# Gated attention followed by an FFT gate, on one core: scores emitted in bursts of four tiles, a halved filter spectrum kept in SBUF, and a tail in borrowed buffers

## The chip, the cores and the metric

The kernel runs on one core of a Trainium2 chip. The metric is the device time of one execution in microseconds (us), as the median of several executions. The unchanged kernel took 1450.63 us (median of 3, 1443.97 to 1451.0) when the prediction was made.

## The reference, cut to what matters

```python
# batch 8, S = 3136 rows (49 * 64), D = 256, d_qk = 64
def attention(u, v, z):
    scores = matmul(z, z.T) / S                 # S x S per batch
    attn = maximum(scores, 0) ** 2
    return u * matmul(attn, v)                  # becomes x

def gate(x, w_proj, filter_fft, w_out):
    x1, x2, x3 = split(x @ w_proj, 3)
    X2 = rfft(x2, n=S, axis=1)
    H = rfft(filter_fft, n=S, axis=0)
    y = x1 * irfft(X2 * H, n=S, axis=1) * x3
    return y @ w_out                            # float32
```

The kernel computes in bf16 with f32 accumulation. Scores are symmetric in z, so they can be made transposed, ready to be multiplied with v. The transform of length 3136 is done as matrix products: a first stage, a second stage, a product with the filter's spectrum, and the way back (stages 3 and 4). The batches are taken in four pairs for it.

## The kernel before

One "chunk" is a group of 384 to 512 output rows of one batch: 8 batches times 7 chunks are 56 chunks. One chunk has 13 "steps". A step makes two 128-row tiles of scores (`scores`), squares the positive part, and multiplies the tiles of some steps earlier with v (`values`) into one accumulator in PSUM, `psout`. At the end of a chunk `finish_chunk` multiplies the accumulator with u into `xT`, and three projections use it. All other work of TensorE (projections, transposes, the transform) is "background": pieces in a queue that are put between the steps.

```python
LAG = 3
class Load:                       # greedy choice of the engine for a piece
    def cost(self, eng, n, fast=1.0):
        if eng == "act": return 150.0 + n / 1.2
        if eng == "dve": return 120.0 + n / 0.96 / fast
        return 200.0 + 2.15 * n
    def take(self, n, engines, fast=1.0):
        best = min(engines, key=lambda e: self.t[e] + self.cost(e, n, fast))
        self.t[best] += self.cost(best, n, fast)
        return best
# ... rring 3 buffers (R), aring 6 (A), psum 3 pairs of banks, psacc 1 (psout) ...

    def stage2(p, kb):            # per block: load y, load the filter's spectrum, multiply
        yl = load_y(y_d[p], kb)
        hl = hld.tile([P, 2, KB * D], BF16, name="hl")
        nc.sync.dma_start(out=hl[:Q2], in_=h_d[:, kb])        # 392 KB
        # ... two matmuls into ps, evicted to xs ...
        nc.vector.tensor_tensor(tt[:Q2], xs[:Q2].unsqueeze(1).to_broadcast(...), hl[:Q2], ALU.mult)

    def scores(b, c, i):
        # ...
            for j in range(2):
                hs = ds(N1 * j, N1)                           # 64 of the 128 rows
                nc.tensor.matmul(ps[:, j, :cw], zT[hs, ds((2 * i + j) * P, P)], zT[hs, ds(s0, cw)],
                                 start=True, stop=True)
        # ...
        if load.take(k * cw, ("act", "dve")) == "act":
            nc.scalar.activation(Rv, pv, AF.Relu)
        else:
            nc.vector.tensor_single_scalar(Rv, pv, 0.0, ALU.max)
        eng = load.take(k * cw, ("act", "dve", "pool"))       # the square
        if eng == "act":
            nc.scalar.activation(Av, Rv, AF.Square)
        else:
            (nc.vector if eng == "dve" else nc.gpsimd).tensor_tensor(Av, Rv, Rv, ALU.mult)
        return A

    inv_s2 = 1.0 / float(S) ** 2
    def finish_chunk(b, c):
        for dh in range(2):       # xT = psout * uT, two DVE operations
            nc.vector.scalar_tensor_tensor(xT[:, dh, :cw], po[:, dh, :cw], inv_s2, uT[:, dh, :cw],
                                           ALU.mult, ALU.mult)

    def plan(b, c):
        # own: the three projections of the chunk just finished, transposes of the next u and z
        # rest: this chunk's share of far (the pieces of the transform)
        for j, f in enumerate(own):
            mixed.append(f)
            lo, hi = j * len(rest) // n, (j + 1) * len(rest) // n
            mixed += rest[lo:hi]
        # ...

    for gi in range(len(steps) + LAG):
        if gi < len(steps):
            amap[steps[gi]] = scores(*steps[gi])
        owed[0] += rate[0]
        while owed[0] >= 1.0 and near:
            near.popleft()()                                  # a background piece
            owed[0] -= 1.0
        # ...
        if gi >= LAG:
            b, c, i = steps[gi - LAG]
            values(b, c, i, amap.pop((b, c, i)))
            if i == NST - 1:
                finish_chunk(b, c)
                while near:
                    near.popleft()()
                plan(b, c)
    # tail: what is left in near and far
```

In the tail, the last pair's transform remains: its whole first stage, stages 2 and 3 in 16 blocks, stages 4 and 5 (load, gate, output projection, store). All loads and stores of the transform go through the SyncE queue.

Of the kernel before, what the change touches and what calls it, by code (L numbers as in the profile page):

```python
# [26 lines left out]
LAG = 3  # L27


class Load:  # L30
# [5 lines left out]
    def cost(self, eng, n, fast=1.0):  # L36
        if eng == "act":
            return 150.0 + n / 1.2
        if eng == "dve":
            return 120.0 + n / 0.96 / fast  # L40
        return 200.0 + 2.15 * n
# [8 lines left out]
def kernel(  # L50
# [37 lines left out]
    h_d = dram.tile([Q2, NKB, 2, KB * D], BF16, name="h_d")  # L88

    const = ctx.enter_context(tc.tile_pool(name="const", bufs=1))  # L90
    zpool = ctx.enter_context(tc.tile_pool(name="zpool", bufs=2))
    zinp = ctx.enter_context(tc.tile_pool(name="zinp", bufs=1))
    uinp = ctx.enter_context(tc.tile_pool(name="uinp", bufs=3))
    utp = ctx.enter_context(tc.tile_pool(name="utp", bufs=2))
    vpool = ctx.enter_context(tc.tile_pool(name="vpool", bufs=9))
    rring = ctx.enter_context(tc.tile_pool(name="rring", bufs=3))
    aring = ctx.enter_context(tc.tile_pool(name="aring", bufs=6))
    psum = ctx.enter_context(tc.tile_pool(name="psum", bufs=3, space=bass.MemoryType.PSUM))
    psacc = ctx.enter_context(tc.tile_pool(name="psacc", bufs=1, space=bass.MemoryType.PSUM))

    def ps_tile():
        return psum.tile([P, 2, 512], F32, tag="ps", name="ps")

# [25 lines left out]
    def load_z(b):  # L129
        zin = zinp.tile([P, NT, dqk], BF16, name="zin")  # L130
        for h, n in split_h(0, NT):
            nc.gpsimd.dma_start(out=zin[ds(N1 * h, N1), 0:n, :], in_=rows_view(z[b], h, 0, n))
        zd = zinp.tile([P, NT, 2, dqk], BF16, name="zd")
        nc.vector.tensor_copy(zd[:, 0:NT - 1], zin[:, 0:NT - 1].unsqueeze(2).to_broadcast([P, NT - 1, 2, dqk]))
        nc.vector.tensor_copy(zd[:N1, NT - 1], zin[:N1, NT - 1].unsqueeze(1).to_broadcast([N1, 2, dqk]))
        zins[b] = zd
        zTs[b] = zpool.tile([P, S], BF16, name="zT")

    def tr_z(b, t0, n):
        zd, zT = zins[b], zTs[b]  # L140
        ps = psum.tile([P, 2048], BF16, tag="ps", name="psz")
        w = 0
        for t in range(t0, t0 + n):
            r = rows_of(t)
            nc.tensor.transpose(ps[:, ds(w, r)], zd[:r, t].rearrange("p a d -> p (a d)"), ident[:r, :r])
            w += r
        evac(zT[:, ds(t0 * P, w)], ps[:, :w], w, fast=2.0)
# [34 lines left out]
    load_z(0)  # L182
    load_v(0, 0)
    load_u(0, 0)
    for q in range(1, 7):
        load_v(0, q)
    wp16 = const.tile([P, 2, 3 * D], BF16, name="wp16")
    nc.gpsimd.dma_start(out=wp16[:], in_=moe_w_proj.rearrange("(t p) n -> p t n", p=P))
    wo16 = const.tile([P, 2, D], BF16, name="wo16")
    nc.gpsimd.dma_start(out=wo16[:], in_=moe_w_out.rearrange("(t p) n -> p t n", p=P))  # L190


    T = const.tile([P, NT, 2, P], BF16, name="T")
    C = const.tile([P, N2, 2, N1], BF16, name="C")
    NTAB = 5
# [5 lines left out]
    with tc.tile_pool(name="tabs", bufs=1) as tabs:  # L201
        pi = tabs.tile([P, 1], I32, name="pi")
        nc.gpsimd.iota(pi[:], pattern=[[0, 1]], base=0, channel_multiplier=1)
        pf = tabs.tile([P, 1], F32, name="pf")
        nc.vector.tensor_copy(pf[:], pi[:])

        def reduced(src, shape, add, name):
            q = tabs.tile(shape, F32, name="q_" + name)
            r = tabs.tile(shape, F32, name="r_" + name)
            if add:  # L210
                nc.vector.tensor_single_scalar(r[:], src, float(add), ALU.add)
                src = r[:]
            nc.vector.tensor_scalar(q[:], src, 1.0 / S, RND, ALU.mult, ALU.add)
            nc.vector.tensor_single_scalar(q[:], q[:], RND, ALU.subtract)
            nc.vector.scalar_tensor_tensor(r[:], q[:], -float(S), src, ALU.mult, ALU.add)
            return r

        ki = tabs.tile([P, NT, N1], I32, name="ki")
        nc.gpsimd.iota(ki[:], pattern=[[0, NT], [1, N1]], base=0, channel_multiplier=0)
        ti = tabs.tile([P, NT, N1], I32, name="ti")  # L220
        nc.gpsimd.iota(ti[:], pattern=[[1, NT], [0, N1]], base=0, channel_multiplier=N2)
        hi = tabs.tile([P, 1], F32, name="hi")
        nc.vector.tensor_single_scalar(hi[:], pf[:], float(N1), ALU.is_ge)
        nc.vector.tensor_single_scalar(hi[:], hi[:], float(HT - N2 * N1), ALU.mult)
        kf = tabs.tile([P, NT * N1], F32, name="kf")
        nc.vector.tensor_copy(kf[:], ki[:].rearrange("p a b -> p (a b)"))
        tf = tabs.tile([P, NT * N1], F32, name="tf")
        nc.vector.tensor_copy(tf[:], ti[:].rearrange("p a b -> p (a b)"))
        nc.vector.scalar_tensor_tensor(kf[:], tf[:], hi[:, 0:1], kf[:], ALU.add, ALU.mult)
        for add, name in ((QUART, "c"), (0, "s")):  # L230
            r = reduced(kf[:], [P, NT * N1], add, name)
            r3 = r[:].rearrange("p (a b) -> p a b", a=NT)
            if add:
                nc.scalar.activation(T[:, :, 0, 0:N1], r3, AF.Sin, scale=SIN_SCALE)
                nc.scalar.activation(T[:, :, 1, N1:P], r3, AF.Sin, scale=SIN_SCALE)
            else:
                nc.scalar.activation(T[:, :, 0, N1:P], r3, AF.Sin, scale=-SIN_SCALE)
                nc.scalar.activation(T[:, :, 1, 0:N1], r3, AF.Sin, scale=SIN_SCALE)


        nf = tabs.tile([P, 1], F32, name="nf")
        nc.vector.tensor_scalar(nf[:], pf[:], 0.5, -0.25, ALU.mult, ALU.add)
        nc.vector.tensor_single_scalar(nf[:], nf[:], RND, ALU.add)
        nc.vector.tensor_single_scalar(nf[:], nf[:], RND, ALU.subtract)
        par = tabs.tile([P, 1], F32, name="par")
        nc.vector.scalar_tensor_tensor(par[:], nf[:], -2.0, pf[:], ALU.mult, ALU.add)
        dpos = tabs.tile([P, 1], F32, name="dpos")
        nc.vector.tensor_single_scalar(dpos[:], par[:], float(QUART), ALU.mult)
        dneg = tabs.tile([P, 1], F32, name="dneg")
        nc.vector.tensor_single_scalar(dneg[:], par[:], -float(QUART), ALU.mult)  # L250
        k2i = tabs.tile([P, N2], I32, name="k2i")
        nc.gpsimd.iota(k2i[:], pattern=[[N1, N2]], base=0, channel_multiplier=0)
        nk = tabs.tile([P, N2], F32, name="nk")
        nc.vector.tensor_copy(nk[:], k2i[:])
        nc.vector.tensor_scalar(nk[:], nk[:], nf[:, 0:1], None, ALU.mult)
        ph = tabs.tile([P, NTAB, N2, 2], F32, name="ph")
        offs = (
# [251 lines left out]


    far = deque()

    def queue_filter():
        filt = {}

# [139 lines left out]
```

## Time and profile before

| | before |
|---|---|
| time, median | 1450.63 us |
| profiled span | 1451.7 us |
| end of the last values matmul | 1293.6 us |
| tail after it | 158.1 us |
| TensorE busy, mean granted clock | 86%, 0.939 |

The first lines are from the profile page of the kernel before: busy time of the engines, then three rows of 40 equal slices of the span, in which a digit is the busy share, the granted TensorE clock, or the DMA share in tenths (9 is 90% or more). PE is TensorE, PEld its weight loads (which overlap PE), DVE is VectorE, ACT ScalarE, POOL GpSimd and SP SyncE.

```profile
span 1451.7 us, 20110 instructions
...
PE 1245.9 (86%) x7379; PEld 562.1 (39%) x7379; DVE 960.5 (66%) x933; ACT 852.7 (59%) x953; POOL 800.7 (55%) x655
...
PE   3888999999988989999989999999999989985643
PEclk8999999999999999999999999999999999995566
DMA  7323543332354625664344725662354535545667
```

There are three stages. In the head TensorE waits for its first data, in the main stage it is busy nearly always, and in the last four slices it is not, at a low clock, while the DMA share rises.

The costliest groups of the page say what TensorE waits for. The columns are line, engine, operation, output<-input, form, count | busy us, mean ns of one | idle us before them, and what ended most of that idle time.

```profile
L496 PE MATMUL psout<-A,vt 128*128 128x512 bf16 (+3 forms) x2800 | 664.0, 359 | 25.2 <-DVE A L483 11.6
...
L465 PE MATMUL ps<-zT 64*128 64x512 bf16 (+2 forms) x1344 | 255.3, 360 | 4.0 <-ACT R L474 1.6
L483 DVE TENSOR_TENSOR A<-R 128x1024 bf16<-128x1024 f32 (+5 forms) x141 | 204.3, 1449 | 81.7 <-ACT R L474 81.4
...
L421 PE MATMUL ps<-xT,wp_142 128*128 128x512 bf16 (+2 forms) x448 | 118.1, 369 | 72.5 <-DVE xT L506 70.0
```

The projections (L421) sat idle for 72.5 us, of which `xT` from DVE ended 70.0 us. No other TensorE group waits that long.

Busy TensorE is not TensorE at its peak. The timeline of the kernel before shows matmuls in order of time: start in us, us, engine, line, operation, tiles, form, how many in a row.

```profile
602.45 0.81 PE L496 MATMUL psout<-A,vt 128*128 128x384 bf16 x4
603.19 0.34 PE L465 MATMUL ps<-zT 64*128 64x384 bf16 x2
603.46 0.51 PE L164 MATMUL psu<-ident,uin 128*128 128x128 bf16 x6
```

The durations overlap, so starts are what counts. Four values matmuls of 384 columns take 4 x 0.163 = 0.65 us between one another, but the score pair starts 0.74 us after the first. The two score matmuls use 64 rows of the array each and run beside each other in 0.17 us, but the next 128-row matmul starts after 0.27 us. Every change between 64-row and 128-row matmuls costs about 0.1 us more than the stream itself. Over the main stage the median extra is 96.5 ns, and in the order of the instructions there are 1415 such changes up to the last values matmul.

The next lines are from the same timeline at the end of a chunk. The number in brackets is idle time before the instruction, and its releaser.

```profile
441.52 0.32 PE L465 MATMUL ps<-zT 64*128 64x384 bf16 x1
443.28 0.34 PE L421 MATMUL ps<-xT,wp_142 128*128 128x384 bf16 x1 [1.44 <-DVE xT L506]
...
444.75 1.49 PE L496 MATMUL psout<-A,vt 128*128 128x384 bf16 x4
...
447.31 1.04 PE L496 MATMUL psout<-A,vt 128*128 128x384 bf16 x4
```

After the last values matmul only one score pair covers the making of `xT`, so TensorE stands still for 1.44 us.

The tail, by window. The columns are stretch, length, then busy us and count for TensorE, weight loads, DVE, ACT, POOL, then granted clock, DMA share, GB/s. The stretches are: to the first second-stage matmul; to the last third-stage matmul; to the first load of stage 4 used; to the end.

```profile
1293.60:1324.10 30.50, 12.50 (x116) 7.58 (x115) 8.79 (x9) 9.04 (x10) 0.00 (x0) 0.68 0.52 141
1324.10:1383.10 59.00, 39.26 (x96) 15.91 (x96) 26.77 (x22) 25.25 (x25) 0.00 (x0) 0.62 0.62 193
1383.10:1388.90 5.80, 0.03 (x1) 0.04 (x1) 0.00 (x0) 1.02 (x1) 0.00 (x0) 0.50 0.28 84
1388.90:1451.70 62.80, 25.18 (x198) 18.41 (x198) 15.18 (x14) 12.87 (x13) 0.00 (x0) 0.69 0.78 193
```

No engine is full in the tail. The first stage of the last pair is still to be done there, the middle loads 392 KB of spectrum per block, and the last part issues all its loads and stores from one queue.

### The profile page before, as it was taken

How to read it: one execution, taken by the hardware profiler on the slowest of the kernel's cores; microseconds unless marked ns; L12 is line 12 of the kernel's file. 1: busy time of each engine (PE TensorE's matmuls, PEld its weight loads, DVE VectorE, ACT ScalarE, POOL GpSimd, SP SyncE). 2: the span in 40 equal slices, each digit the busy share in tenths (PEclk: the TensorE clock that was granted, in tenths of full speed). 3: DMA queues.
4: the chain of work that ended last, by engine and by line, in shares of the span. 5: the costliest groups of instructions: out<-in, count | busy, mean ns of one | idle time of the engine just before them, and what ended most of it. 6: DMA issues, size and time to landing. Idle time of an engine off the chain costs nothing. (4 is left out here: it accounts for less than half of the span.)

```text
span 1451.7 us, 20110 instructions
## 1 busy us (share of the span) xinstructions
PE 1245.9 (86%) x7379; PEld 562.1 (39%) x7379; DVE 960.5 (66%) x933; ACT 852.7 (59%) x953; POOL 800.7 (55%) x655
## 2 busy tenths in 40 slices
PE   3888999999988989999989999999999989985643
PEld 1233433443343334543334334543344334542222
DVE  7766677667767776667767766676777866653421
ACT  3655666666665556666666656666666656653421
POOL 8656765576555655556656855565566755530000
PEclk8999999999999999999999999999999999995566
DMA  7323543332354625664344725662354535545667
GB/s 119 70 65 79 141 118 94 91 64 51 85 137 121 144 75 142 150 128 89 99 122 132 177 69 144 157 140 64 92 136 136 140 97 143 136 106 176 204 170 182
DMA packets 164900, 173.69 MB, mean 120 GB/s; under 512 B 18496, under 2 KB 119040, under 8 KB 164800
## 3 DMA queue, kind: packets, MB, share of 16 engines
q1 hardware_dynamic: 144656, 141.35, 34.3%
q0 software_dynamic: 20144, 31.05, 14.7%
q8 instruction: 58, 0.95, 0.3%
q14 instruction: 42, 0.34, 0.1%
HBM read 129.50 MB, written 73.86 MB: 140 GB/s over the span
## 5 line engine op out<-in xcount | busy, mean ns | idle before, releaser
L483 POOL TENSOR_TENSOR A<-R 128x768 bf16<-128x768 f32 (+3 forms) x398 | 663.4, 1673 | 426.9 <-ACT R L474 262.1
L496 PE MATMUL psout<-A,vt 128*128 128x512 bf16 (+3 forms) x2800 | 664.0, 359 | 25.2 <-DVE A L483 11.6
L474 ACT ACTIVATE R<-ps 128x1024 f32<-128x1024 f32 (+4 forms) x474 | 416.1, 886 | 275.7 <-PE ps L465 229.6
L496 PEld LDWEIGHTS <-vt 128*128 128x128 bf16 (+1 forms) x2800 | 251.3, 99 | 267.2 <-issue 97.6
L476 DVE TENSOR_SCALAR R<-ps 128x1024 f32<-128x1024 f32 (+3 forms) x254 | 264.7, 1048 | 125.4 <-PE ps L465 107.0
L465 PE MATMUL ps<-zT 64*128 64x512 bf16 (+2 forms) x1344 | 255.3, 360 | 4.0 <-ACT R L474 1.6
L483 DVE TENSOR_TENSOR A<-R 128x1024 bf16<-128x1024 f32 (+5 forms) x141 | 204.3, 1449 | 81.7 <-ACT R L474 81.4
L481 ACT ACTIVATE A<-R 128x1024 bf16<-128x1024 f32 (+4 forms) x189 | 177.8, 941 | 89.6 <-DVE R L476 87.0
L421 PE MATMUL ps<-xT,wp_142 128*128 128x512 bf16 (+2 forms) x448 | 118.1, 369 | 72.5 <-DVE xT L506 70.0
L465 PEld LDWEIGHTS <-zT 64*128 64x128 bf16 x1344 | 67.0, 93 | 249.6 <-issue 243.5
L351 DVE TENSOR_TENSOR tt<-xs,hl 98x2048 bf16<-98x2048 bf16 x64 | 100.2, 1567 | 48.9 <-ACT xs L108 43.3
L388 DVE TENSOR_TENSOR yT<-ps,gl 128x1024 bf16<-128x1024 f32 x48 | 58.7, 1222 | 57.4 <-DMA gl<-g_d_64 31.5
L153 POOL DMA_DIRECT2D uin<-in_u_dram x112 | 63.9, 573 | 44.0 <-PE psu L164 37.5
L421 PEld LDWEIGHTS <-wp_142 128*128 128x128 bf16 x448 | 38.7, 99 | 117.3 <-DVE xT L506 59.6
L360 PE MATMUL ps<-tt,FT 98*98 98x512 bf16 x256 | 80.6, 443 | 4.0 <-DVE tt L351 4.0
L108 ACT ACTIVATE ve<-ps 98x1024 bf16<-98x1024 f32 x49 | 50.0, 1021 | 35.8 <-PE ps L360 35.4
L506 DVE SCALAR_TENSOR_TENSOR xT<-psout,uT 128x512 bf16<-128x512 f32 (+2 forms) x112 | 64.8, 615 | 8.3 <-PE psout L496 8.2
L347 PE MATMUL ps<-yl,FT 98*98 98x512 bf16 x128 | 46.8, 449 | 26.2 <-DMA yl<-y_d_68 24.3
L108 ACT ACTIVATE xs<-ps 98x1024 bf16<-98x1024 f32 x45 | 46.0, 1021 | 38.6 <-PE ps L347 38.3
L108 ACT ACTIVATE ot<-ps 128x1024 f32<-128x1024 f32 (+1 forms) x35 | 34.5, 985 | 56.4 <-PE ps L404 20.9
L404 PE MATMUL ps<-wo_144,yT 128*128 128x256 bf16 (+1 forms) x400 | 57.0, 285 | 11.5 <-DVE yT L393 7.1
L174 POOL DMA_DIRECT2D vt<-in_v_dram x104 | 56.9, 554 | 15.3 <-PE ps L465 11.5
(324 smaller groups left out, 935.9 us busy)
## 6 DMA issues: line engine op xcount, KB each, us to landing
hl<-h_d SPq DMA_DIRECT2D x64, 392.0 KB
out_dram<-ot SPq DMA_DIRECT2D x192, 128.0 KB
vt<-in_v_dram POOLq DMA_DIRECT2D x96, 128.0 KB, 4.4
uin<-in_u_dram POOLq DMA_DIRECT2D x56, 128.0 KB, 3.5
h_d<-hl SPq DMA_DIRECT2D x16, 392.0 KB
uin<-in_u_dram POOLq DMA_DIRECT2D x56, 96.0 KB, 2.9
yl<-y_d_69 SPq DMA_DIRECT2D x16, 196.0 KB
yl<-y_d_65 SPq DMA_DIRECT2D x16, 196.0 KB
```

The lines of the kernel that those rows point to most:

```text
L108: nc.scalar.activation(dst, src, AF.Copy)
L153: nc.gpsimd.dma_start(out=uin[ds(N1 * h, N1), 0:m, :], in_=rows_view(u[b], h, t0, m))
L351: nc.vector.tensor_tensor(tt[:Q2], xs[:Q2].unsqueeze(1).to_broadcast([Q2, 2, KB * D]), hl[:Q2], ALU.mult)
L360: nc.tensor.matmul(ps[:Q2, j, :], m, tt[:Q2, i, ds(j * 512, 512)], start=(i == 0), stop=(i == 1))
L421: nc.tensor.matmul(ps[:, nb, :cw], wp16[:, ks, ds((2 * comp + nb) * P, P)], xT[:, ks, :cw], start=(ks == 0), stop=(ks == 1))
L465: nc.tensor.matmul(ps[:, j, :cw], zT[hs, ds((2 * i + j) * P, P)], zT[hs, ds(s0, cw)], start=True, stop=True)
L474: nc.scalar.activation(Rv, pv, AF.Relu)
L476: nc.vector.tensor_single_scalar(Rv, pv, 0.0, ALU.max)
L481: nc.scalar.activation(Av, Rv, AF.Square)
L483: (nc.vector if eng == "dve" else nc.gpsimd).tensor_tensor(Av, Rv, Rv, ALU.mult)
L496: nc.tensor.matmul(po[:, dh, :cw], vts[b, kt // 4][:r, kt % 4, ds(dh * P, P)], A[:r, kt - 2 * i, :cw], start=(kt == 0), stop=(kt == NT - 1))
L506: nc.vector.scalar_tensor_tensor(xT[:, dh, :cw], po[:, dh, :cw], inv_s2, uT[:, dh, :cw], ALU.mult, ALU.mult)
```

## The change

The intent has five parts.

1. Scores are emitted two steps at a time (four tiles), then two values steps, so that TensorE changes between 64-row and 128-row matmuls half as often. `LAG` goes from 3 to 4, the ring of `A` from 6 to 8 buffers.
2. At a chunk end, transform pieces come ahead of the projections. Squares are no longer given to DVE.
3. The spectrum of the real filter is symmetric, so only half of it is made (9 blocks for 16). It stays in SBUF, and is read backwards through three extra tables.
4. The first stage of a pair's transform is done chunk by chunk, as soon as the chunk's projection is there. The tables are made behind the first chunk's scores, where they stood ahead of them.
5. In the tail, loads go through POOL's queue into buffers of the attention that are free by then, and `psout` serves as a fourth PSUM buffer.

The core of the diff (cuts marked with `# ...`):

```diff
-LAG = 3
+LAG = 4
+NH = N1 // 2 + 1
# ... cost(): act 150 -> 190 + n/1.2, dve 120 -> 150 + n/0.96
# ... pools: uinp 3 -> 2, vpool 9 -> 8, x2p 17 -> 10, aring 6 -> 8, gp 2 -> 3, no h_d, no x1p
+    tail = {"on": False, "n": 0}
     def ps_tile():
+        if tail["on"]:
+            tail["n"] += 1
+            if tail["n"] % 4 == 0:
+                return psacc.tile([P, 2, 512], F32, name="psout")
         return psum.tile([P, 2, 512], F32, tag="ps", name="ps")
+    def buf(shape, dtype, own, name, lent):
+        if tail["on"]:
+            p, tag = lent
+            return p.tile(shape, dtype, tag=tag, name=name)
+        return late[own].tile(shape, dtype, name=name)
+    def dma_in(**kw):
+        (nc.gpsimd if tail["on"] else nc.sync).dma_start(**kw)
# ... tables() is now a function and the last piece of the first plan; T, FT changed
     def stage2(p, kb):
-        hl = hld.tile([P, 2, KB * D], BF16, name="hl")
-        nc.sync.dma_start(out=hl[:Q2], in_=h_d[:, kb])
# ...
-        nc.vector.tensor_tensor(tt[:Q2], xs[:Q2]..., hl[:Q2], ALU.mult)
+        nc.vector.tensor_tensor(tt[:Q2], xs[:Q2]..., late["H"][:Q2, :, ds(a0, KB), :]..., ALU.mult)
# ... scores():
-        eng = load.take(k * cw, ("act", "dve", "pool"))
+        eng = load.take(k * cw, ("act", "pool"))
# ... plan(): the share of the transform is put ahead of each own piece
-        for j, f in enumerate(own):
-            mixed.append(f)
-            lo, hi = j * len(rest) // n, (j + 1) * len(rest) // n
-            mixed += rest[lo:hi]
+        for j in range(n):
+            hi = -(-(j + 1) * len(rest) // n)
+            near.extend(rest[done:hi])
+            done = hi
+            near.extend(own[j:j + 1])
# ... own also gets first_stage(b, c) for the second batch of a pair
-    for gi in range(len(steps) + LAG):
-        if gi < len(steps):
-            amap[steps[gi]] = scores(*steps[gi])
# ...
+    for g0 in range(0, total + LAG, 2):
+        for s in (g0, g0 + 1):
+            if s < total:
+                amap[s] = scores(*steps[s])
+        vs = [s for s in (g0 - LAG, g0 + 1 - LAG) if 0 <= s < total]
+        if len(vs) == 2 and steps[vs[1]][2] == NST - 1:
+            vs.reverse()
+        if vs and steps[vs[0]][2] != NST - 1 or not vs:
+            background(1.0)
+        for j, s in enumerate(vs):
+            # ... values(); at a chunk's last one finish_chunk, rest of near, plan
+            if j == 0:
+                background(1.0)
+    tail["on"] = True
```

## The prediction

> **What bounds it now.** TensorE, in three stages (per-slice and window views). Head, 0 to 44 us: PE mostly waits for tables and first squares. Main, 44 to 1294 us: PE busy 46 to 47 of 50 us, clock 0.98. Tail, 1294 to 1451 us: 157 us, PE at most 60% busy, clock 0.61 to 0.67.
>
> I split the main stage's 1250 us by start-to-start times of matmuls (timeline). Streaming (N/2.4 ns plus 2.5): 965 us. Mode changes: a 64-row score matmul starts 312 ns after a values matmul instead of 216 (N=512), 258 instead of 163 (N=384); the way back costs 103 ns more than its stream. The Trainium skill, "TensorEngine Tiling (Array Packing)", Key Properties, says that changing the tiling mode drains the array; the trace agrees, at about 100 ns a change. Some 1,400 changes: 140 us. Waits: 145 us, of which 69 us is the first projection waiting for xT at 56 chunk ends (costliest groups: 72.5 us idle there, released by xT). The other 76 us includes the clock.
>
> **What the change does.**
>
> 1. Two score steps in a row, then two values steps; stage-1 pieces often follow scores. By instruction order, mode changes fall from 1,418 to 892. 526 x 0.1 us = **-52 us**, all critical.
> 2. At a chunk end, four score matmuls and a background piece (0.9 us) stand between the last values matmul and the first user of xT, where one score pair stood. An xT takes two DVE operations of 0.55 to 0.68 us. 69 falls to 20 us: **-49 us**.
> 3. Streaming is unchanged: half the filter's second stage goes (-7 us), pair 3's first stage moves in from the tail (+5 us).
> 4. DVE loses its 141 squares (204 us) but takes back relus; ACT, DVE and POOL carry 700 to 940 us each, 65 to 80% of the shorter main stage. Three PSUM pairs serve bursts of two scores: **+10 to +30 us** of new short waits.
> 5. Head: tables come behind the first chunk, first scores need half of z. Table-making (20 us of DVE) still blocks the filter's first stage: **-5 us**.
> 6. Tail: the first stage (23 us) shrinks to two units. Stage 2/3 took 65 us, waiting 2.4 to 4.9 us for y loads behind 392 KB spectrum loads; without them, with eight load buffers, a chain of about 2.3 us a block: 40 us. In stage 4/5 (66 us) the SP queue issues almost without a gap (100 issues of 0.4 to 0.75 us). Half move to POOL. The skill, "DMA: Bandwidth & Descriptors", Issuing engines are not separate DMA queues, says spreading issues only saves sequencer time; engines are already 76% busy, so 12 us comes. Tail 157 to 112: **-45 us**.
>
> **Prediction.** 1450 - 52 - 49 + 20 - 5 - 45 = 1319, say 1315 us. Range 1270 to 1350. Faster by over 2%: 0.96; within: 0.03; slower: 0.01.
>
> **What would show it.** Right: score groups of four with one pair of changes; idle before the first projection under 25 us; values end near 1200 us; tail 105 to 120 us, DMA share above 0.8 in its second half. Wrong: PE idle before background matmuls released by evictions over 100 us; values waiting for POOL squares; POOL's in-order queue stuck on load issues.
>
> **What would make it wrong.** PSUM turnover eating the saved drains; the xT wait moving to the next values matmul, which needs the one accumulator; a lower clock.

## The result, and the profile after

| | before | after |
|---|---|---|
| time, median of the same rounds | 1449.78 us (1443.97 to 1451.0, 4 runs) | 1298.0 us (1296.0 to 1299.69, 4 runs) |
| profiled span | 1451.7 us | 1294.2 us |
| last values matmul ends | 1293.6 us | 1185.7 us |
| tail | 158.1 us | 108.5 us |
| mean granted clock | 0.939 | 0.965 |

The ratio is 0.896, with a 95% interval of 0.8931 to 0.8989. Ratios here are the mean time of one kernel's fast runs over that of the other's fast runs of the same rounds, so they are not quite the ratio of the medians quoted.

The same lines of the profile page, of the kernel after:

```profile
span 1294.2 us, 19775 instructions
...
PE 1164.2 (90%) x7285; PEld 553.6 (43%) x7349; DVE 888.5 (69%) x936; ACT 845.4 (65%) x954; POOL 844.1 (65%) x746
...
PE   6499999999999989999999999999999989997754
PEclk9699999999999999999999999999999999999677
DMA  8144342225233455667223456667222445655548
```

This trace lacks 64 of 7349 matmul records, as the two counts for PE and PEld show. Counts of mode changes below are therefore taken from the order of the instructions. The costliest groups of the kernel after, with the same columns as before:

```profile
L541 PE MATMUL psout<-A,vt 128*128 128x512 bf16 (+4 forms) x2750 | 643.7, 355 | 27.1 <-DVE xT L551 23.5
...
L508 PE MATMUL ps<-zT 64*128 64x512 bf16 (+2 forms) x1344 | 197.4, 358 | 15.0 <-DVE R L519 10.5
...
L464 PE MATMUL ps<-xT,wp_167 128*128 128x384 bf16 (+2 forms) x430 | 104.9, 356 | 11.0 <-ACT R L517 3.3
```

The wait of the projections went from 72.5 to 11.0 us, and `xT` is no longer what ends most of it. The values matmuls now wait 23.5 us for `xT`, but 13.0 us of that is one single wait in the head, told of below. The scores wait a little more for relus, 15.0 us where they waited 4.0.

The timeline of the kernel after:

```profile
608.40 0.61 PE L508 MATMUL ps<-zT 64*128 64x512 bf16 x4
608.94 1.04 PE L541 MATMUL psout<-A,vt 128*128 128x512 bf16 x4
```

Four score matmuls now share one way in and one way out. From the first of them to the values matmul is 0.54 us: two pairs of 0.216 us, and once 0.1 us. The size of a drain is as it was (median extra 95.5 ns), but the number up to the last values matmul is 888 where it was 1415.

The tail after, with the windows and columns as before:

```profile
1185.70:1198.20 12.50, 4.16 (x31) 1.98 (x30) 3.18 (x5) 2.79 (x4) 8.59 (x14) 0.82 0.72 216
1198.20:1240.90 42.70, 32.81 (x96) 15.04 (x96) 23.89 (x20) 26.44 (x27) 10.88 (x18) 0.73 0.51 157
1240.90:1247.80 6.90, 0.04 (x1) 0.04 (x1) 0.00 (x0) 1.02 (x1) 2.66 (x4) 0.54 0.22 69
1247.80:1294.20 46.40, 24.88 (x198) 19.10 (x198) 15.18 (x14) 12.88 (x13) 19.45 (x28) 0.72 0.80 216
```

Three parts gave 18.0, 16.3 and 16.4 us, and the short gap between them cost 1.1 us.

The two spans differ by 157.5 us, and the parts of that are:

| part | before to after |
|---|---|
| streaming of matmuls up to the last values (from shapes and counts; of the kernel after in a complete trace, that of the run `after_tailsp`) | -2 us |
| mode changes, 1415 to 888 at 0.0965 us | -51 us |
| all other stalls up to the last values, waits and half clock (what is left of the difference) | -54 us |
| first matmul, 7.6 to 6.7 us | -1 us |
| tail | -50 us |

The third row is the net of several. Idle time of TensorE in the main stage (from the end of the second chunk) waiting for `xT` went from 71.6 to 12.9 us, idle time for all else from 21 to 34 us, and time at half clock from 51 to 10 us, which is worth about half of that in work, 20 us. These come to some 66 us, more than the row, since the terms overlap. In the head there is a new wait of 13 us, but up to the second `xT` the head as a whole is only 1.2 us longer (77.4 us for 76.2).

### The profile page after: what moved, and what is told of

It reads as the page before. It is cut to its first block, busy times and chain, and to the rows that moved or that the text cites. A ratio compares the mean times of both kernels' runs of the same rounds, so it can differ in the third digit from the quotient of the medians.

```text
span 1294.2 us, 19775 instructions
## 1 busy us (share of the span) xinstructions
PE 1164.2 (90%) x7285; PEld 553.6 (43%) x7349; DVE 888.5 (69%) x936; ACT 845.4 (65%) x954; POOL 844.1 (65%) x746
## 4 chain that ended last, share of the span: by engine, by line
PE 39%; DVE 5%; DMA 4%; POOL 3%; issue 3%; ACT 2%; SPq 1%; DVEq 0%; ACTq 0%; POOLq 0%
PE psout L541 18%; PE ps L508 5%; PE ps L464 4%; PE ps L403 2%; POOL A L526 2%; PE ps L490 2%; PE ps L447 2%; DVE R L519 2%; PE ps L389 1%; PE ps L352 1%; PE ps L427 1%; PE psu L193 1%; DVE xT L551 1%; DMA out_dram<-ot 1%; POOL vt L203 1%
## 5 line engine op out<-in xcount | busy, mean ns | idle before, releaser
L541 PE MATMUL psout<-A,vt 128*128 128x512 bf16 (+4 forms) x2750 | 643.7, 355 | 27.1 <-DVE xT L551 23.5
L519 DVE TENSOR_SCALAR R<-ps 128x1024 f32<-128x1024 f32 (+4 forms) x338 | 353.6, 1059 | 179.6 <-PE ps L508 134.7
L517 ACT ACTIVATE R<-ps 128x1024 f32<-128x1024 f32 (+3 forms) x390 | 334.4, 879 | 189.6 <-PE ps L508 153.6
L524 ACT ACTIVATE A<-R 128x1024 bf16<-128x1024 f32 (+4 forms) x323 | 302.5, 939 | 107.5 <-DVE R L519 102.0
L508 PE MATMUL ps<-zT 64*128 64x512 bf16 (+2 forms) x1344 | 197.4, 358 | 15.0 <-DVE R L519 10.5
L393 DVE TENSOR_TENSOR tt<-xs,H 98x2048 bf16<-98x2048 bf16 x64 | 92.7, 1453 | 38.2 <-ACT xs L132 37.1
L464 PE MATMUL ps<-xT,wp_167 128*128 128x384 bf16 (+2 forms) x430 | 104.9, 356 | 11.0 <-ACT R L517 3.3
L479 DVE TENSOR_TENSOR g<-ps,g 128x1024 bf16<-128x1024 f32 (+2 forms) x56 | 60.9, 1088 | 19.9 <-PE ps L464 12.2
L551 DVE SCALAR_TENSOR_TENSOR xT<-psout,uT 128x512 bf16<-128x512 f32 (+2 forms) x112 | 64.2, 613 | 4.3 <-PE psout L541 3.8
L136 DVE CAST ye<-ps 128x1024 bf16<-128x1024 f32 (+2 forms) x44 | 44.2, 1008 | 19.5 <-PE ps L352 19.2
L490 PE MATMUL ps<-wp_167,xT 128*128 128x256 bf16 (+1 forms) x400 | 54.0, 273 | 0.7 <-DVE xT L551 0.7
```

The lines of the kernel that those rows point to most:

```text
L136: nc.vector.tensor_copy(dst, src)
L464: nc.tensor.matmul(ps[:, nb, :cw], wp16[:, ks, ds((2 * comp + nb) * P, P)], xT[:, ks, :cw], start=(ks == 0), stop=(ks == 1))
L490: nc.tensor.matmul(ps[:r, i // 2, ds((i % 2) * D, D)], xT[:, ks, ds(i * P, r)], wp16[:, ks, D:2 * D], start=(ks == 0), stop=(ks == 1))
L541: nc.tensor.matmul(po[:, dh, :cw], vts[b, kt // 4][:r, kt % 4, ds(dh * P, P)], A[:r, kt - 2 * i, :cw], start=first_of and kt == kts[0], st ...
```

## The experiments

The question is not only whether the change is faster but which part gives what. My theory was the prediction's: the mode changes are all on the critical path, the background ahead of the projections covers the making of `xT`, and the engines behind are not critical. The general rival was that the parts do not add: what one removes, another wait takes.

Two figures carry the accounting. "Idle" is TensorE's idle time (gaps over 0.15 us) in the main stage, from the end of the second chunk to the last values matmul. "Half clock" is the time of that stage at a granted clock of 0.5; all clock records there are either 0.5 or 1.0. How long `xT` takes is given from the end of the chunk's last values matmul to the end of `xT`, as a mean from the third chunk on.

The kernel before was run again in the rounds of every experiment (medians 1446.8 to 1452.0 us). The kernel after was not: "more than the kernel after" means more than the 1298.0 us of its own rounds, so a difference of a few us there should not be leaned on. The "37 us" of some expectations is the part of the main stage's gain that I could not place at that time.

### Bursts alone, on the kernel before

```diff
-LAG = 3
+LAG = 4
-    for gi in range(len(steps) + LAG):
-        if gi < len(steps):
-            amap[steps[gi]] = scores(*steps[gi])
-        # background, values(gi - LAG)
+    for g0 in range(0, len(steps) + LAG, 2):
+        for gi in (g0, g0 + 1):
+            if gi < len(steps):
+                amap[steps[gi]] = scores(*steps[gi])
+        for gi in (g0, g0 + 1):
+            # background, values(gi - LAG), as before
```

> The kernel before with one thing changed: two score steps, then two values steps (lag 4 for 3); its background order, its tail, its engine choice are kept. By instruction order it has 920 mode changes where before has 1,418. Theory (a mode change drains the array and costs 0.1 us): 50 us less from the changes and about 10 us less xT wait, since one more score pair stands before the first projection: about 1390 us. Rival (the gain of the change comes from its order of background work and its tail, pairing alone only moves the waits): 1430 us or more.

It took 1455.97 us, ratio 1.0043 (1.0023 to 1.0063): no gain at all. The mode changes fell to 917 as planned, which is worth 48 us. Idle rose from 93 to 118 us and half clock from 51 to 82 us. The projections' line of this kernel's groups shows the main part of it:

```profile
L421 PE MATMUL ps<-xT,wp 128*128 128x512 bf16 (+2 forms) x448 | 126.1, 394 | 85.9 <-DVE xT L506 80.0
```

The theory that saved drains are all critical fell here. A burst alone makes the waits longer: `xT` was ready 2439 ns after the last values matmul on average, against 2037 ns in the kernel before. I had overlooked one reason. A chunk has 13 steps, so with two values steps in a row every second chunk ends on the first of the two, and its projection is emitted directly behind its last values matmul, with no score matmul between. Those chunk ends waited 52.8 us for `xT` (34.5 in the kernel before), the others 30.0 (37.8). So the gain that I had expected came at every second chunk end only, and was more than lost at the rest. Waits for other things than `xT` grew too, from 21 to 36 us.

### Scores over all 128 rows, on the kernel before

This takes the mode changes away without touching the order. `zT` holds z twice, on rows 0 to 63 and 64 to 127, so contracting over all rows gives twice the score, and the square four times it.

```diff
-                hs = ds(N1 * j, N1)
-                nc.tensor.matmul(ps[:, j, :cw], zT[hs, ds((2 * i + j) * P, P)], zT[hs, ds(s0, cw)],
+                nc.tensor.matmul(ps[:, j, :cw], zT[:, ds((2 * i + j) * P, P)], zT[:, ds(s0, cw)],
-    inv_s2 = 1.0 / float(S) ** 2
+    inv_s2 = 0.25 / float(S) ** 2
```

> The kernel before, but each score matmul contracts over all 128 rows: z already stands twice in the 128 partitions, so the scores come out doubled and the final scale is divided by 4; the result stays right. Score pairs no longer run side by side, which adds about 128 us of streaming on PE; mode changes fall from 1,418 to 280. Theory (0.1 us a change): 114 us less for the changes, so in sum about 14 us more than before, 1450 to 1475 us. Rival (the extra 100 ns between a values matmul and a score matmul is an artefact of the records, or overlaps other waits): the full 128 us shows, about 1560 to 1580 us.

It took 1443.78 us, ratio 0.9961 (0.9943 to 0.9978). The score matmuls no longer run beside each other, so their stream doubles, and the kernel is still a little faster. The timeline of this kernel at the place shown above:

```profile
602.96 0.81 PE L495 MATMUL psout<-A,vt 128*128 128x384 bf16 x4
603.61 0.49 PE L464 MATMUL ps<-zT 128*128 128x384 bf16 x2
603.93 1.04 PE L404 MATMUL ps<-wo,yT 128*128 128x256 bf16 x8
```

The scores now start 0.65 us after the values (0.74 before), and take 0.32 us for two, one behind the other (0.27 for two beside each other). So a drain of about 0.1 us each way is real. As an estimate, the streams grow by 125 us (672 pairs, 0.187 us each at the mean width of 448 columns), and 1138 fewer changes (277 left) take 110 us away. That alone would make it 15 us longer. What turns it into a gain is less waiting: idle fell from 93 to 71 us and half clock from 51 to 31 us. Running two 64-row matmuls side by side gained next to nothing when every pair paid for two changes. The Trainium skill, "TensorEngine Tiling (Array Packing)", Key Properties, says that a change of tiling mode drains TensorE. These runs agree, and give it a size.

### Transform pieces ahead of the projections, on the kernel before

```diff
         for j, f in enumerate(own):
-            mixed.append(f)
-            lo, hi = j * len(rest) // n, (j + 1) * len(rest) // n
+            lo, hi = -(-j * len(rest) // n), -(-(j + 1) * len(rest) // n)
             mixed += rest[lo:hi]
+            mixed.append(f)
```

> The kernel before with one swap: within a chunk each share of the background pieces is put ahead of the chunk's own piece (projection) instead of behind it, so that a background piece stands between the last values matmul and the first projection. One score step at a time, 1,374 mode changes. Theory (the wait for xT at chunk ends costs its idle time and, on top, clock: after such waits the array runs at half clock for a while, 51 us of the main stage of before): xT idle 72 us falls to about 20, half-clock time to about 20 us: 1375 to 1395 us. Rival (the wait only moves to the next values matmul, which needs the one accumulator that xT reads): 1440 us or more.

It took 1418.34 us (1410.57 to 1422.7), ratio 0.9783 (0.9748 to 0.9819). The projections' line of this kernel:

```profile
L421 PE MATMUL ps<-xT,wp 128*128 128x512 bf16 (+2 forms) x448 | 113.8, 368 | 16.8 <-DVE xT L506 9.4
```

The wait of the projections nearly went, from 72.5 to 16.8 us. But the whole gain was 31 us, less than I had expected: waits for `xT` at all users were still 31 us in the main stage, since the next chunk's values need the accumulator that `xT` frees.

### No squares on DVE, on the kernel before

```diff
-        eng = load.take(k * cw, ("act", "dve", "pool"))
+        eng = load.take(k * cw, ("act", "pool"))
```

> The kernel before with one word changed: squares may go to ACT and POOL only, no longer to DVE. Emission, background order, tail as before; about 1,400 mode changes. On the changed kernel the reverse edit cost 69 us. Theory (a square on DVE waits in DVE's in-order queue for a relu on ACT, 81 us in the kernel before, and holds up evictions and xT behind it; this is the 37 us of the main stage that pairing, background order and tail leave open): 1400 to 1420 us, half-clock time in the main stage below 30 us for 51. Rival (it hurts only beside bursts of two scores): within 8 us of 1449 us.

It took 1429.91 us (1426.27 to 1431.85), ratio 0.9847 (0.9815 to 0.9878). `xT` was ready after 1814 ns (2037 before), idle fell from 93 to 82 us and half clock from 51 to 27 us. Alone it gives 22 us.

### One step at a time, on the kernel after

```diff
-    for g0 in range(0, total + LAG, 2):
-        # two score steps, background, two values steps with background between
+    for g in range(total + LAG):
+        if g < total:
+            amap[g] = scores(*steps[g])
+        background(1.0)
+        s = g - LAG
+        # values(s); at a chunk's last one finish_chunk, rest of near, plan
```

> The changed kernel with the emission undone: one score step, background, one values step; all else kept (lag 4, background first at a chunk end, spectrum in SBUF, tail). Mode changes 1,392 for 892. Theory: 50 us more for the changes, and about 10 us more xT wait because one score pair fewer stands before its user: about 1355 us. Rival (pairing is worth nothing once the rest is there): within 10 us of 1298 us.

It took 1329.0 us, ratio 0.9169 (0.9149 to 0.9188): 31 us more than the kernel after, not 57. The mode changes are 1387, which costs 48 us. Idle is 33 us, though, 14 less than with bursts. So bursts also have a price in the kernel after: about a third of what they save goes back into short waits.

### Projections ahead of the transform pieces, on the kernel after

```diff
+            near.extend(own[j:j + 1])
             near.extend(rest[done:hi])
             done = hi
-            near.extend(own[j:j + 1])
```

> The changed kernel with one swap: in each chunk the projections come ahead of the other background pieces instead of behind the first of them. Theory (the background piece between the last values matmul and the first user of xT hides the xT latency): the idle time of PE waiting for xT in the main stage rises from 13 us to about 45 us, total about 1330 us. Rival (the four score matmuls alone hide it): within 8 us of 1298 us.

It took 1354.92 us, ratio 0.9338 (0.9305 to 0.9372), 57 us more than the kernel after. The projections' line of this kernel:

```profile
L464 PE MATMUL ps<-xT,wp 128*128 128x512 bf16 (+2 forms) x444 | 117.0, 368 | 78.7 <-DVE xT L551 74.2
```

The wait for `xT` is back at the size that it had before the change, although the bursts and the free DVE are still there. `xT` is ready after 1870 ns here and 1918 ns in the kernel after, so the making of it is not what changed. What stands in front of its user is. Idle rises by 39 us, half clock from 10 to 55 us.

It is not the same at all chunk ends, which decides between theory and rival. TensorE's timeline of this kernel at two chunk ends, one after the other:

```profile
479.40 0.35 PE L464 MATMUL ps<-xT,wp 128*128 128x448 bf16 x1 [2.63 <-DVE xT L551]
...
503.81 0.61 PE L508 MATMUL ps<-zT 64*128 64x512 bf16 x4
504.66 0.38 PE L464 MATMUL ps<-xT,wp 128*128 128x512 bf16 x1 [0.24 <-DVE xT L551]
```

At every second chunk end (the first line) the swap puts the projection directly behind the last values matmul, and the score matmuls come after it. There the wait for `xT` rose from 6.3 us in all, in the kernel after, to 51.6 us. At the others (the last two lines) four score matmuls still stand between, and without the background piece the wait rose only from 7.3 to 11.1 us. So where the four score matmuls stand they hide nearly all of the wait alone, as the rival said. Where nothing stands the whole of it shows. So the 57 us are for the most part the price of an uncovered end at every second chunk, and not of the background piece as such.

### Both undone, on the kernel after

The edit is the last two together.

> The changed kernel with both undone: one score step at a time, and projections ahead of background pieces. Pairing alone gained nothing on the kernel before, and 31 us on the changed one. Theory (pairing pays only where the chunk ends are covered; where they are not, burstier waits and half-clock time give its 50 us back): about 1355 us, the same as with pairing and projections first (1355). Rival (the two gains add up): about 1355 + 31 = 1386 us.

It took 1369.22 us, ratio 0.9461 (0.9443 to 0.9479), between the two expectations. With the projections first, the bursts are worth 14 us; with the transform pieces first, 31 us. The parts do interact.

### Squares on DVE again, on the kernel after

```diff
-        eng = load.take(k * cw, ("act", "pool"))
+        eng = load.take(k * cw, ("act", "dve", "pool"))
```

> The changed kernel with squares allowed on DVE again, as in the kernel before; else the same. Theory (the engines beside PE are off the critical path at 65 to 75% busy): within 6 us of 1298 us. Rival (squares on DVE held up the relus and xT on DVE, and taking them off explains the 37 us of the main stage that are open): 1315 us or more, with more half-clock time than 10 us in the main stage.

It took 1367.01 us (1359.14 to 1368.72), ratio 0.9418 (0.9382 to 0.9453): 69 us more, where I had expected at most 6. This is the largest effect of any single line, though the line also deals out the relus anew: in the main stage ACT does 467 of them (379 in the kernel after) and DVE 231 (319). The mode changes are the same (886 in all, against 892). Idle is 90 us (47 in the kernel after), half clock 58 us (10). `xT` is ready after 2504 ns (1918), and 13 times it ran directly behind a square in DVE's queue (7 times in the kernel before, never in the kernel after). Of the 43 us more of idle time, 16 us are waits for `xT` itself; 19 us are for other results of DVE, relus and evictions above all, and 10 us for ACT. The loss is spread: comparing chunk by chunk, the offset grows steadily from 4 to 71 us. The DVE squares in this kernel's groups:

```profile
L526 DVE TENSOR_TENSOR A<-R 128x1024 bf16<-128x1024 f32 (+5 forms) x155 | 240.6, 1556 | 112.3 <-ACT R L517 111.3
```

Two things in the traces say why a square on DVE costs so much. First, a square takes its input from ACT in many cases, and DVE waits for it 111.3 us with everything else behind it. The Trainium skill, "TensorE: Matmul & The Clock Gate", in its part on the array's sub-arrays and queue depths, says that ACT and DVE are strict FIFO, and these waits agree. Second, the square is slowed by POOL. In the kernel before, a square of 128x1024 on DVE takes 1.22 us when POOL is idle, and a median of 2.06 us (4.46 at most) when a POOL square runs beside it for at least half of that time; a relu that reads PSUM takes 1.22 us either way. The skill, "SBUF — State Buffer", Who interferes with whom, says that a DVE instruction with two SBUF inputs contends with a GpSimd instruction that reads SBUF. The trace agrees. Here is one case of the kernel before, first in DVE's timeline:

```profile
464.63 4.52 DVE L483 TENSOR_TENSOR A<-R 128x896 bf16<-128x896 f32 x1 [0.17 <-ACT R L474]
469.07 1.21 DVE L351 TENSOR_TENSOR tt<-xs,hl 98x2048 bf16<-98x2048 bf16 x1
470.21 1.01 DVE L506 SCALAR_TENSOR_TENSOR xT<-psout,uT 128x384 bf16<-128x384 f32 x2
```

POOL's timeline of the same kernel, beside it:

```profile
464.86 3.33 POOL L483 TENSOR_TENSOR A<-R 128x896 bf16<-128x896 f32 x2
```

And TensorE's timeline of the same kernel, behind it:

```profile
470.81 0.82 PE L421 MATMUL ps<-xT,wp_142 128*128 128x384 bf16 x2 [5.21 <-DVE xT L506]
```

The square took 4.52 us, close to the 3.33 us of the two POOL squares plus the 1.08 us that this shape takes alone. The two operations behind it, `xT` among them, came late, TensorE stood still for 5.21 us, and within that wait a stretch of 6.8 us at half clock began. As an estimate from the durations of the kernel with DVE squares, POOL stretches them by some 68 us in all, beside the 111.3 us that DVE waits for their relus. Which of the two, the place in the queue or the shared port, carries more of the 69 us is not separated by a run, and stays open, as does what the other dealing of the relus adds.

### The tail with nothing borrowed, and with its queue moved back

```diff
-    tail["on"] = True
```

> The changed kernel with the tail switch never set: tail loads on the SP queue, own two or three buffers, three PSUM pairs. No spectrum reload, first stage per chunk stay. Theory (before, the last stage of the tail was held by the SP queue, which issued 100 transfers in 64 us): last two stages take 61 us again instead of 46, and the middle ones some 48 instead of 44: tail about 130 us for 108.5, total about 1318 us. Rival (the tail's gain is all from the spectrum and the per-chunk first stage): within 6 us of 1298 us.

```diff
     def dma_in(**kw):
-        (nc.gpsimd if tail["on"] else nc.sync).dma_start(**kw)
+        nc.sync.dma_start(**kw)
```

> The changed kernel, tail buffers borrowed as there, but the tail's loads issued by the SP queue as in the kernel before. Theory (it is the queue's issue time that counts): nearly all of the tail switch's gain is gone, about 1313 us. Rival (it is the buffers that count): below 1303 us.

The first took 1312.48 us, ratio 0.9067 (0.9048 to 0.9086); the second 1303.99 us, ratio 0.901 (0.8992 to 0.9027). Only the last part of the tail moved much. It is 46.4 us in the kernel after, 54.9 us with all loads on SyncE's queue, and 64.2 us with the buffers given back as well:

```profile
1245.90:1310.10 64.20, 28.66 (x198) 20.11 (x198) 15.18 (x14) 12.85 (x13) 0.00 (x0) 0.66 0.75 188
```

So the queue is worth some 8.5 us and the borrowed buffers (with the fourth PSUM buffer) some 9.3 us, nearly in equal parts. For the queue alone the theory expected more and the rival less. SyncE's own timeline shows what the queue does. In the kernel before its issues of loads and stores alternate almost without a gap (SPq in the third column is SyncE's sequencer, which issues them):

```profile
1414.55 7.98 SPq L411 DMA_DIRECT2D out_dram<-ot  x12
1422.58 0.59 SPq L372 DMA_DIRECT2D vl<-v_d_73  x1
1423.27 0.44 SPq L376 DMA_DIRECT2D gl<-g_d_63  x1
```

Loads wait behind a row of 12 stores. In the kernel after this queue has the stores alone:

```profile
1254.54 37.02 SPq L454 DMA_DIRECT2D out_dram<-ot  x50
```

The skill, "DMA: Bandwidth & Descriptors", Issuing engines are not separate DMA queues, says that issuing on several engines saves only the sequencer's time, which is usually small against the transfer. Here 81 issues (43.5 us of SyncE's sequencer) in one queue became 50 (28.6 us) beside 31 on POOL (22.1 us), and that was worth 8.5 of 55 us. But the loads also no longer stand behind stores that wait for their data, and no run separates this from the sequencer's time.

### The spectrum loaded again, on the kernel after

A load of 392 KB into `tt` ahead of each of the 64 products stands for the loads that the change removed. The product overwrites what was loaded, so the result stays right.

```diff
         tt = buf([P, 2, KB * D], BF16, "tpp", "tt", (rring, "R"))
+        dma_in(out=tt[:Q2]..., in_=y_d[NP]...[:, ds((kb % 8) * 2 * KB, 2 * KB), :])   # 392 KB
```

> The changed kernel with a load of 392 KB (98 rows of 4 KB) put back in front of each of the 64 spectrum products, into the product's own tile, so that the product waits for it; the values loaded are not used and the result stays right. Theory (the spectrum reload cost nothing in the main stage, where DMA engines are half idle, but time in the tail, where each y load stood behind one): values end within 5 us of 1186 us, the middle part of the tail grows from 44 us to about 60, total about 1315 us. Rival (the reloads cost the main stage too, and explain the 37 us of it that pairing, background order and tail leave unexplained): values end 20 us or more later, total over 1330 us.

It took 1307.79 us (1302.98 to 1311.35), ratio 0.9017 (0.898 to 0.9053). That interval still touches the one of the kernel after (0.8931 to 0.8989), so the time alone is not decisive. In the trace the values end 4 us later (1189.8 us) and the tail is 8 us longer (116.4 us), of which 6 us are in its middle part. So these loads matter in the tail and hardly in the main stage. The middle part of the tail shrank by 16.3 us with the change; 6 us of that are explained by the loads, and 10 us are not explained by any run. It is not the borrowed buffers or POOL's queue, since the middle part takes 41.6 us with neither (`after_tailoff`). The run here also sends its loads through POOL's queue in the tail, and so does not bring back what the kernel before had, a spectrum load in SyncE's queue ahead of each load of y (its second stage waited 24.3 us for y). That case is untested.

### A try at a better version: tables in pieces behind two chunks

In the kernel after, the making of the tables sits on DVE just when the first chunk ends. DVE's timeline of the kernel after:

```profile
44.28 0.98 DVE L248 TENSOR_SCALAR r<-kf 128x1600 f32<-128x1600 f32 x1
45.18 0.68 DVE L551 SCALAR_TENSOR_TENSOR xT<-psout,uT 128x512 bf16<-128x512 f32 x1
45.78 0.97 DVE L250 TENSOR_SCALAR q<-r 128x1600 f32<-128x1600 f32 x1
46.68 0.68 DVE L551 SCALAR_TENSOR_TENSOR xT<-psout,uT 128x512 bf16<-128x512 f32 x1
```

TensorE's timeline of the kernel after, at the same time:

```profile
47.41 5.87 PE L541 MATMUL psout<-A,vt 128*128 128x512 bf16 x20 [13.04 <-DVE xT L551]
```

The experiment cuts the tables in six pieces, of which the later ones go between the projections of the first chunk, and starts the filter one chunk later.

```diff
+    table_steps = tables()            # now a generator with yields between the pieces
+    def more_tables():
+        next(table_steps, None)
# plan(): first plan
-            own.append(tables)
+            own.append(more_tables)
# plan(): after the first chunk
+            own = [more_tables, own[0], more_tables, own[1], more_tables, *own[2:], more_tables, more_tables]
```

> A version meant to beat both: the changed kernel with its table-making cut in six pieces, which stand between the second chunk's other work (its integer ramps a chunk earlier), the filter's first stage one chunk later, and the tables' DVE and ACT time counted in the engine choice. Theory (in the head PE waits 13 us because xT of the first chunk stands behind the tables on DVE, and 5 us more for the tables): xT of the first chunk is done at about 36 us instead of 47, of the second at about 63 instead of 77, total about 1285 us. Rival (the head's DVE work is the limit wherever it stands): 1295 us or more.

It took 1312.48 us (1310.34 to 1316.93), ratio 0.9056 (0.9027 to 0.9086), slower than the kernel after. The head did gain: `xT` of the first chunk was ready at 38.3 us (47.4), of the second at 69.6 us (77.4). Between about the 18th and the 40th chunk this was lost again and more, with half clock 22 us (10). The greedy choice of engines had been given other loads at the start and so distributed the later pieces otherwise. That this is the cause is argued, not shown. No run here beat the kernel after.

### The accounts of the main stage put together

For each kernel, the difference of the main stage's length to its base, and what three terms give: mode changes times 0.0965 us, idle, and half of the time at half clock. The terms overlap a little (a stretch at half clock may hold idle time), so the sum is an estimate.

| against | kernel | changes | idle | half clock / 2 | sum | measured |
|---|---|---|---|---|---|---|
| before | after | -51 | -46 | -20 | -118 | -109 |
| before | bursts alone | -48 | +24 | +15 | -9 | +2 |
| before | transform pieces first | -4 | -28 | -7 | -39 | -33 |
| before | no DVE squares | 0 | -11 | -12 | -23 | -25 |
| after | single steps | +48 | -14 | -2 | +32 | +29 |
| after | projections first | +2 | +39 | +22 | +63 | +57 |
| after | both of these | +49 | +30 | +7 | +86 | +72 |
| after | DVE squares | 0 | +43 | +24 | +67 | +70 |

Three single edits of the kernel before give +6, -31 and -22 us, together -47, where the change gives -109 in the main stage. Undoing them in the kernel after costs 31, 57 and 69 us, together 157. I read it so: a wait is the making of `xT` minus what covers it, and never less than nothing, so the last part that is missing costs much more than the first one gives. That is argued from the traces; no run tests it apart.

## Why the prediction was right or wrong

The prediction was 1315 us (1270 to 1350), and the kernel took 1298.0 us. Point by point:

1. "526 x 0.1 us = -52 us, all critical." The count and the size were right (1415 to 888 up to the last values; 96 ns each; the run with full rows confirms the drain). "All critical" was wrong as a statement about this part. Alone the bursts gave nothing, in part since they leave every second chunk end uncovered, and in the kernel after they are worth 31 us, since they bring short waits of their own.
2. "69 falls to 20 us: -49 us." It fell by 59 us, from 71.6 to 12.9. The mechanism was right: it is the cover, as the run with projections first shows (the wait of their line went back to 78.7 us), and not a faster `xT` (2037 to 1918 ns). In that run nearly all of the wait came back at the chunk ends where nothing stood in front of the projection. Where the four score matmuls stood it stayed small without the background piece (11.1 us for 7.3), so there the scores alone were nearly enough. What is left moved in part, as the prediction had feared: 10.5 of the 12.9 us are now in front of values matmuls, which need the one accumulator. The prediction had left the clock inside "the other 76 us" and had no term for its fall with these waits: half clock went from 51 to 10 us, some 20 us.
3. "Streaming is unchanged." -2 us; right.
4. "DVE loses its 141 squares ... +10 to +30 us of new short waits." Idle time for other things than `xT` rose from 21 to 34 us, as predicted. The failed step is the reading of DVE as an engine with room, whose squares do not matter. Putting them back costs 69 us, and taking them out of the kernel before gains 22 us. A 66% share of busy time said nothing about an in-order queue with `xT` in it.
5. "Head: ... -5 us." This failed. The second chunk's `xT` was ready at 77.4 us, and at 76.2 before. The tables moved off the start, and the first `xT` came earlier (47.4 us for 54.2), but they then stood on DVE in front of it: 13.0 us of wait.
6. "Tail 157 to 112: -45 us." It fell by 50 us, to 108.5. The first stage gave 18.0 us, the middle 16.3, the last part 16.4, of which the queue is some 8.5 (the prediction had 12 for it) and the borrowed buffers some 9.3, as the two tail runs show by the part's length.

"Score groups of four", "idle before the first projection under 25 us" (11.0) and "tail 105 to 120 us" (108.5) were all seen, and values end was near 1200 us (1185.7). "DMA share above 0.8 in its second half" was not seen: the share was 0.80 in the last part and 0.22 in the short gap before it.

The terms of the prediction add up to -131 us: -81 in the main stage, -5 in the head, -45 in the tail. The two profiled executions differ by -157.5 us: -109, +1 and -50. In the main stage the terms that came out better are the `xT` wait (10 us), its clock (20 us, no term) and the short waits (13 for 20, so 7 us). They overlap, so their sum of 37 us is more than the 28 us to be explained. So the main path of the prediction was right: fewer mode changes, a covered `xT`, a shorter tail. That the total came so near owes something to luck. Judged by the runs that undo one thing, the bursts were worth 31 us and not 52, and the squares taken off DVE, which the prediction booked as a source of new waits, were worth 69 us.

## What to carry to other kernels

Ask at each wait of the bottleneck engine how long the thing waited for takes to make, and what stands in front of its user, at every place where it is used: one order of the pieces that left nothing there at every second chunk end cost 57 us here, without making anything slower. Look at what else stands in the queue of the engine that makes what the bottleneck waits for, whatever its share of busy time: here squares that waited for another engine and ran longer beside POOL cost 22 to 69 us. Judge a part of such a change by undoing it in the new kernel as well as by doing it alone in the old one, since the two answers can differ by a factor of three.

## What the Trainium skill lacked or had wrong

- "TensorEngine Tiling (Array Packing)", Key Properties, says that a mode change drains TensorE but gives no cost. Here it is a median of 96.5 ns a change beyond the stream in the kernel before and 95.5 ns in the kernel after. At that price, pairs of 64-row matmuls beside each other gain next to nothing when each pair pays for two changes (ratio 0.9961 for full rows, against half rows).
- "TensorE: Matmul & The Clock Gate", Part 1, gives two clock states and a window of 3413 ns, with the slow state "after ≥1 idle window (~3.4µs)". The records of the main stage agree with the states (0.5 and 1.0 only) and with the lengths (3.413 or 6.827 us). But single gaps of 1.44 us (at 443 us), 1.71 us and 1.8 us in the kernel before were already followed by a stretch at half clock, so gaps well below a window can be enough. The changes of the clock there lie on one grid of 3.413 us. In the kernel before, the 12 windows of this grid at full clock that half clock followed held 1.44 to 3.17 us of idle time; of the other windows at full clock one held 1.70 us, in two gaps, and none of the rest over 1.38. In the kernel after the border is less sharp: 1.36 us was followed by half clock, and 1.68 us was not.
- "DMA: Bandwidth & Descriptors", Issuing engines are not separate DMA queues, calls the issue time saved usually small. With many small transfers, giving the loads a second queue was worth 8.5 of 54.9 us in the last part of the tail, the loads' place behind the stores included.
- "SBUF — State Buffer", Who interferes with whom, has a rule for two SBUF inputs beside a GpSimd operation that these traces agree with. It gives no size for tensor_tensor beside a row of GpSimd operations: a DVE square took 4.52 us where that shape takes 1.08 us alone, beside two POOL squares of 3.33 us together. The DVE square had started 0.23 us before them and was still the one that grew; POOL's squares of 128x1024 took a median of 1.89 us in the kernel before, with a DVE square beside them and with none of DVE's two-input operations (records on POOL are rough).
